# Fewer and longer dummy matmuls, an earlier first chunk, and a scale group moved into a K step, in the opening of a DiT block

## The chip, the cores and the metric

One core of one Trainium2 chip. The metric is the time of one execution in device microseconds. Timed runs come in rounds with the kernel before on the same chip.

## The reference

A DiT block with adaptive layer norm; only its first lines matter here.

```python
B, N, D = 2, 256, 1152
mod = (_silu(c) @ w_mod).reshape(B, 6, 1, D)
shift_a, scale_a, gate_a, shift_m, scale_m, gate_m = [mod[:, i] for i in range(6)]
h = _layernorm(x, axis=-1) * (1 + scale_a) + shift_a
qkv = (h @ wqkv).reshape(B, N, 3, H, Dh)
# [...] attention, wo, gated residual, second layer norm, MLP
```

## The kernel before

Tokens are four tiles of 128 (tiles 0 and 1 are batch 0, tiles 2 and 3 are batch 1). The opening normalizes them, transposes them on the tensor engine in chunks of 128 features ("chunk k"), multiplies each chunk by its scale (hT0), and accumulates six panels of K chunk by chunk ("K step k"). The scales come from small matmuls ("scale groups") on columns of w_mod that arrive by transfers in five pieces. Dummy matmuls on zeros keep the tensor engine busy until data is there.

```python
    zeros = const.tile([P, T], BF16, name="zeros")          # T = 512
    nc.vector.memset(zeros[:], 0.0)
    # [...]
    SGROUPS = [(0, 2), (2, 4), (4, 6), (6, 8), (8, 9)]
    for k0, k1 in SGROUPS:                # transfers, in this order on one queue
        nc.sync.dma_start(w_scale_a[:, :, k0 * P:k1 * P], ...)
        for a, z in [(0, 1), (1, 2)] if k0 == 0 else [(k0, k1)]:
            load_k(a, z, 0, KM1 * P)      # rows of w_k
    # [...]
    zeros32 = zeros[:].bitcast(FP32)      # 256 fp32 columns
    def warm(n, dst):
        for _ in range(n):
            nc.tensor.matmul(dst[:, 0:T // 2], zeros32[:, 0:P], zeros32, start=True, stop=True)
    warm(2, pwarm)
    nc.tensor.transpose(pc[:], c_sb[:], ident[0:B * KD, 0:B * KD])     # c, for the silu
    # [...]
    warm(8, pwarm)
    # [...] statistics: tiles 0 and 2 on ScalarE, 1 and 3 on VectorE
    pm0, pm1 = [scale_group(k, k + 1, acc_tile) for k in range(2)]
    act_var(2)                                                         # VectorE
    nc.vector.tensor_scalar_mul(hT0[:, 0, 0:N], pt_a[:, 0, :], pm0[:, 0, 0:1])
    scale_add(pm1, 1, 2, "a")
    modulate(pt_a, 1, 1, 0, 0, "d")
    ln_exp_rsqrt(rstd1[:, 2:3], mv1[:, 2, 1:2])                        # ScalarE
    nc.scalar.copy(scale_a[:, 0:1, :], pm0[:])
    norm1(2, 0, CUT)                                                   # VectorE
    # [...]
    k_step(0, 0, N)                        # K step 0, batch 0: six 128x256
    transpose_x([0, 1], [2], pt_c, 0)      # tile 2, chunks 0 and 1
    k_step(1, 0, N)
    modulate(pt_c, 0, 0, 1, 0, "d")        # chunk 0 of batch 1
    # [...]
    k_step(0, N, T)                        # K step 0, batch 1
    pm = scale_group(2, 4)
    # [...]
    for k in range(3, KD):
        if k in (3, 5, 7):
            k1 = min(k + 3, KD)
            scale_add(scale_group(k + 1, k1), k + 1, k1)
        if k < KD - 1:
            both(transpose_x([k + 1], range(NT)), k + 1)   # VectorE, then ScalarE
        k_step(k)                          # six 128x512
```

## Time and profile before

| | before |
|---|---|
| timed runs, median (lowest to highest) | 243.22 us (243.17 to 243.69), 3 runs |
| the profiled execution | 244.21 us, span 242.4 us |
| tensor engine busy | 98% of the span |
| its wait for w_scale_a columns 6-7 | 0.64 us |
| that transfer: issued, landed | 11.08 us, 19.77 us |

The page of the kernel before: its busy line, and the chain that ended last (shares of the span, by engine and by line).

```profile
span 242.4 us, 3999 instructions
...
PE 237.1 (98%) x1701; PEld 145.0 (60%) x1701; DVE 91.4 (38%) x193; ACT 59.6 (25%) x120; POOL 28.9 (12%) x48
...
PE 91%; SPq 4%; DMA 4%; issue 0%; DVE 0%; DVEq 0%
```

The chain is tensor work except for 8%: a transfer and the queue that issued it. The table of waits of the tensor engine in the first 30 us (waiting line, releaser: total us, times, longest; here its two longest) names the place.

```profile
PE pwarm L173 <- DVE eps_t L93: 1.2, 1, 1.2
PE pm L245 <- DMA w_scale_a<-in_w_mod_dram: 0.6, 1, 0.6
```

The timeline of the tensor engine of the kernel before (start, duration, line, operation, count, idle time before it). L173 are the dummies, L262 transposes, L278 K steps, L245 scale groups. It is put together from three stretches; the last, from 17.3 us, was asked up to 22.6 us, so its last line counts three of six matmuls.

```profile
1.18 2.07 PE L173 MATMUL pwarm<-zeros 128*128 128x256 f32 x4 [1.18 <-DVE eps_t L93]
3.18 0.19 PE L176 MATMUL pc<-ident,c_sb 18*128 18x18 bf16 x1
3.30 5.14 PE L173 MATMUL pwarm<-zeros 128*128 128x256 f32 x16
8.63 0.38 PE L262 MATMUL pt<-ident,xn 128*128 128x128 bf16 x4 [0.19 <-ACT xn L204]
...
10.42 0.82 PE L278 MATMUL pk<-big,w_k 128*128 128x256 bf16 x6
11.22 0.28 PE L262 MATMUL pt<-ident,xn 128*128 128x128 bf16 x2
11.34 1.49 PE L278 MATMUL pk<-big,w_k 128*128 128x256 bf16 x12
12.67 0.59 PE L245 MATMUL pm<-sT,w_scale_a 128*128 128x2 bf16 x18
...
17.73 1.46 PE L278 MATMUL pk<-big,w_k 128*128 128x512 bf16 x6
19.82 0.60 PE L245 MATMUL pm<-sT,w_scale_a 128*128 128x2 bf16 x18 [0.64 <-DMA w_scale_a<-in_w_mod_dram]
20.29 0.38 PE L262 MATMUL pt<-ident,xn 128*128 128x128 bf16 x4
20.50 1.46 PE L278 MATMUL pk<-big,w_k 128*128 128x512 bf16 x6
21.80 0.39 PE L262 MATMUL pt<-ident,xn 128*128 128x128 bf16 x4
22.02 0.81 PE L278 MATMUL pk<-big,w_k 128*128 128x512 bf16 x3
```

From 10.42 to 12.67 (the second scale group) nothing waits. The wait at 19.82 is the one that the change aims at. Last, the transfer of columns 6-7 in the view of transfers (size, us from issue to landing):

```profile
w_scale_a<-in_w_mod_dram SPq DMA_DIRECT2D x1, 576.0 KB, 8.7
```

### The profile page before, as it was taken

How to read it: one execution, taken by the hardware profiler on the slowest of the kernel's cores; microseconds unless marked ns; L12 is line 12 of the kernel's file. 1: busy time of each engine (PE TensorE's matmuls, PEld its weight loads, DVE VectorE, ACT ScalarE, POOL GpSimd, SP SyncE). 2: the span in 40 equal slices, each digit the busy share in tenths (PEclk: the TensorE clock that was granted, in tenths of full speed). 3: DMA queues.
4: the chain of work that ended last, by engine and by line, in shares of the span. 5: the costliest groups of instructions: out<-in, count | busy, mean ns of one | idle time of the engine just before them, and what ended most of it. 6: DMA issues, size and time to landing. Idle time of an engine off the chain costs nothing.

```text
span 242.4 us, 3999 instructions
## 1 busy us (share of the span) xinstructions
PE 237.1 (98%) x1701; PEld 145.0 (60%) x1701; DVE 91.4 (38%) x193; ACT 59.6 (25%) x120; POOL 28.9 (12%) x48
## 2 busy tenths in 40 slices
PE   8998999999999999999999999999999999999994
PEld 5675454465567665888854444444656656655674
DVE  4742442318416578831002999960010000000001
ACT  6622332307215032671422233322000000000000
POOL 2400000001400333200000000001121111111111
PEclk9999999999999999999999999999999999999999
DMA  6999999996499999239999999999300000000000
GB/s 184 325 317 318 376 366 391 390 392 236 107 314 398 388 374 145 40 62 351 390 391 392 342 327 290 271 326 286 97 16 16 20 16 16 20 16 17 29 22 16
DMA packets 48781, 53.29 MB, mean 220 GB/s; under 512 B 9587, under 2 KB 36475, under 8 KB 48763
## 3 DMA queue, kind: packets, MB, share of 16 engines
q1 hardware_dynamic: 41312, 50.14, 62.2%
q10 hardware_dynamic: 6939, 1.71, 5.1%
q0 software_dynamic: 512, 1.19, 1.8%
q8 instruction: 13, 0.21, 0.4%
q14 instruction: 5, 0.04, 0.1%
HBM read 50.14 MB, written 1.19 MB: 212 GB/s over the span
## 4 chain that ended last, share of the span: by engine, by line
PE 91%; SPq 4%; DMA 4%; issue 0%; DVE 0%; DVEq 0%
PE pacc L732 29%; PE pacc L788 29%; PE pacc L679 7%; PE pacc L588 7%; PE pq L510 7%; DMA w_scale_a<-in_w_mod_dram 4%; SPq L104 3%; PE pk L307 2%; PE pk L278 2%; PE pa L628 2%; PE ps_s L545 2%; PE pn L405 2%; SPq L86 1%; SPq L107 1%; PE pg L487 0%; PE pm L245 0%
## 5 line engine op out<-in xcount | busy, mean ns | idle before, releaser
L732 PE MATMUL pacc<-hT,w_f 128*128 128x256 bf16 (+1 forms) x432 | 70.5, 326 | 0.0
L788 PE MATMUL pacc<-w_f,gT 128*128 128x384 bf16 (+2 forms) x468 | 70.5, 314 | 0.0
L788 PEld LDWEIGHTS <-gT 128*128 128x128 bf16 x468 | 44.4, 98 | 26.3
L732 PEld LDWEIGHTS <-w_f 128*128 128x128 bf16 x432 | 42.2, 98 | 27.6
L794 DVE TENSOR_TENSOR tmp<-pacc,gate 128x384 f32<-128x384 f32 (+2 forms) x13 | 6.9, 527 | 65.6 <-PE pacc L788 57.2
L764 ACT ACTIVATE gT<-pacc 128x512 bf16<-128x512 f32 x24 | 14.3, 597 | 32.6 <-PE pacc L732 32.6
L458 DVE SCALAR_TENSOR_TENSOR part<-w_gate_m,s,part 128x1152 f32<-128x1152 bf16 x16 | 21.4, 1412 | 0.0
L796 POOL TENSOR_TENSOR o_sb<-tmp,x 128x384 bf16<-128x384 f32 (+1 forms) x12 | 11.7, 972 | 54.1 <-DVE tmp L794 54.1
L679 PE MATMUL pacc<-w_o,big 128*128 128x384 bf16 x108 | 17.9, 326 | 0.0
L510 PE MATMUL pq<-hT,w_q 128*128 128x512 bf16 x81 | 17.8, 379 | 0.0
L588 PE MATMUL pacc<-w_v,hT 128*128 128x384 bf16 x108 | 17.7, 326 | 0.0
L588 PEld LDWEIGHTS <-hT 128*128 128x128 bf16 x108 | 10.5, 98 | 7.1 <-issue 0.3
L679 PEld LDWEIGHTS <-big 128*128 128x128 bf16 x108 | 10.4, 98 | 7.2 <-issue 0.4
L510 PEld LDWEIGHTS <-w_q 128*128 128x128 bf16 x81 | 7.8, 97 | 9.5
L278 PE MATMUL pk<-big,w_k 128*128 128x256 bf16 (+1 forms) x72 | 13.2, 326 | 0.0
L685 POOL TENSOR_TENSOR x<-tmp,x_sb 128x384 f32<-128x384 f32 x8 | 7.3, 913 | 27.1 <-DMA w_scale_m<-in_w_mod_dram 15.2
L456 DVE TENSOR_SCALAR part<-w_gate_m,s 128x1152 f32<-128x1152 bf16 x2 | 1.6, 818 | 22.1 <-DMA w_gate_m<-in_w_mod_dram 22.1
L480 POOL DMA_DIRECT2D gates_dram<-nat_v x2 | 1.1, 536 | 67.7 <-DVE nat_v L478 67.7
L278 PEld LDWEIGHTS <-w_k 128*128 128x128 bf16 x72 | 6.7, 98 | 3.7 <-issue 0.3
L753 ACT ACTIVATE gT<-pacc 128x512 bf16<-128x512 f32 x12 | 6.5, 598 | 9.1 <-PE pacc L732 9.1
L173 PE MATMUL pwarm<-zeros 128*128 128x256 f32 x20 | 7.2, 527 | 1.2 <-DVE eps_t L93 1.2
L501 POOL DMA_DIRECT2D gates_dram<-nat x4 | 2.3, 586 | 50.6 <-DVE nat L498 49.9
(101 smaller groups left out, 165.9 us busy)
## 6 DMA issues: line engine op xcount, KB each, us to landing
w_f<-in_w_fc_dram SPq DMA_DIRECT2D x12, 864.0 KB, 14.6
w_f<-in_w_fc_dram SPq DMA_DIRECT2D x3, 1728.0 KB, 7.8
w_f<-in_w_fc_dram SPq DMA_DIRECT2D x2, 2592.0 KB, 17.2
w_gate_a<-in_w_mod_dram SPq DMA_DIRECT2D x3, 864.0 KB, 11.8
w_v<-in_wqkv_dram SPq DMA_DIRECT2D x3, 864.0 KB, 13.9
w_o<-in_wo_dram SPq DMA_DIRECT2D x3, 864.0 KB, 14.0
w_shift_m<-in_w_mod_dram SPq DMA_DIRECT2D x3, 864.0 KB, 8.6
w_scale_m<-in_w_mod_dram SPq DMA_DIRECT2D x3, 864.0 KB, 13.4
```

Of the source, the lines that this page charges most:

```text
L104: nc.sync.dma_start(w_k[:, k0:k1, c0:c1], wqkv_v[:, k0:k1, D + c0:D + c1])
L173: nc.tensor.matmul(dst[:, 0:T // 2], zeros32[:, 0:P], zeros32, start=True, stop=True)
L278: nc.tensor.matmul(pk[m][:, c0:c1], w_k[:, k, m * P:(m + 1) * P], hT0[:, k, c0:c1], start=(k == 0 and c0 == 0), stop=(k == KD - 1), skip_g ...
L458: nc.vector.scalar_tensor_tensor(part[:, b, :], wg[:, k, :], s32[:, k, b:b + 1], part[:, b, :], op0=ALU.mult, op1=ALU.add,)
L510: nc.tensor.matmul(pq[m][:], w_q[:, k, m * P:(m + 1) * P], hT[:, k, :], start=(k == 0), stop=(k == KD - 1), skip_group_check=True,)
L588: nc.tensor.matmul(pacc[:], hT[:, k, t * P:(t + 1) * P], w_v[:, k, pnl * PW:(pnl + 1) * PW], start=(k == 0), stop=(k == KD - 1),)
L679: nc.tensor.matmul(pacc[:], aT[:, k, t * P:(t + 1) * P], w_o[:, k, c0:c1], start=(k == 0), stop=(k == KD - 1),)
L685: (nc.gpsimd if pool_add else nc.vector).tensor_tensor(x1[:, t, c0:c1], tmp[:], x_sb[:, t, c0:c1], op=ALU.add)
L732: nc.tensor.matmul(dst, w_f1[m // KD][:, k, ml * P:(ml + 1) * P], hT[:, k, c0:c1], start=start, stop=(k == KD - 1), **kw,)
L764: nc.scalar.activation(gT[:, m, :], pacc[:], ACT.Gelu_apprx_tanh)
L788: nc.tensor.matmul(pacc[:], gT[:, kk, t * P:(t + 1) * P], w_f2[j][:, r, c0 - n * PW:c0 - n * PW + cw], start=(kk == 0), stop=(kk == KF - 1),)
L796: (nc.vector if last else nc.gpsimd).tensor_tensor(o_sb[:], tmp[:], x1[:, t, c0:c0 + cw], op=ALU.add)
```

## The change

Three parts, all in the opening. Five fp32 dummies of 512 columns in place of ten of 256. Chunk 0 of batch 0 multiplied ahead of tile 2's variance on VectorE, which idled there; with it, tile 2's transposes go behind K step 1. Two matmuls of K step 5 ahead of scale group 6-7, to fill the wait for its transfer.

```diff
-    zeros = const.tile([P, T], BF16, name="zeros")
-    nc.vector.memset(zeros[:], 0.0)
+    zeros32 = const.tile([P, T], FP32, name="zeros32")
+    nc.vector.memset(zeros32[:], 0.0)
+    zeros = zeros32[:, 0:T // 2].bitcast(BF16)
 [...]
-            nc.tensor.matmul(dst[:, 0:T // 2], zeros32[:, 0:P], zeros32, start=True, stop=True)
-    warm(2, pwarm)
+            nc.tensor.matmul(dst[:], zeros32[:, 0:P], zeros32[:], start=True, stop=True)
+    warm(1, pwarm)
 [...]
-    warm(8, pwarm)
+    warm(4, pwarm)
 [...]
+    nc.vector.tensor_scalar_mul(hT0[:, 0, 0:N], pt_a[:, 0, :], pm0[:, 0, 0:1])
     act_var(2)
-    nc.vector.tensor_scalar_mul(hT0[:, 0, 0:N], pt_a[:, 0, :], pm0[:, 0, 0:1])
 [...]
     k_step(0, 0, N)
+    k_step(1, 0, N)
     transpose_x([0, 1], [2], pt_c, 0)
-    k_step(1, 0, N)
 [...]
     for k in range(3, KD):
+        split = 2 if k == 5 else 0
+        k_step(k, 0, T, 0, split)
         if k in (3, 5, 7):
 [...]
-        k_step(k)
+        k_step(k, 0, T, split, KM1)
```

More of the change, by code (lines that the diff above doesn't have):

```diff
@@ L166 @@
     pwarm = acc_tile([P, T], "pwarm")
-    zeros32 = zeros[:].bitcast(FP32)
     def warm(n, dst):
         for _ in range(n):
-            nc.tensor.matmul(dst[:, 0:T // 2], zeros32[:, 0:P], zeros32, start=True, stop=True)
-    warm(2, pwarm)
+            nc.tensor.matmul(dst[:], zeros32[:, 0:P], zeros32[:], start=True, stop=True)
+    warm(1, pwarm)
     nc.tensor.transpose(pc[:], c_sb[:], ident[0:B * KD, 0:B * KD])
@@ L320, in fill @@
         for _ in range(n):
-            nc.tensor.matmul(pwarm[:], zeros[:, 0:P], zeros[:], start=True, stop=True)
+            nc.tensor.matmul(pwarm[:], zeros[:, 0:P], zeros, start=True, stop=True)
     def pool_eps(t):
```

## The prediction

> **What bounds the kernel.** The tensor engine: PE is 98% busy on the page, and the chain of waits, followed back, is unbroken tensor work from 19.82 us to 239.3. Before that it leaves the engine: 8.69 us for the transfer of w_scale_a columns 6-7 (issued 11.08, landed 19.77), and the transfer queue's issues before it. The table of waits gives the tensor engine 0.64 us idle there (timeline: K step 4 ends near 19.18, scale group 6-7 starts 19.82). So time saved before 19.2 us only lengthens this wait; only what moves work into it is gained.
>
> **What the change does.**
>
> 1. Dummies. Ten fp32 128x256 become five 128x512: the same columns. In the trace each is two records, 0.427 us apart at first and 0.216 us from about 6.5 us on. This agrees with the Trainium skill, "TensorE: Matmul & The Clock Gate", Part 1: half-rate clock until a free-running window of about 3.4 us was busy. The zero tile now has 512 fp32 words, not 256. Its memset took 0.27 us; I estimate 0.54, so the first dummy starts near 1.45, not 1.18, and the transpose of c, behind one long dummy, 0.1-0.15 us later; batch 0's statistics slip as much. Worth nothing by itself.
>
> 2. Chunk 0 ahead of tile 2's variance. VectorE idled 0.58 us before that variance (9.94; it waits for ScalarE until 9.91); chunk 0's multiply started at 10.02. It can start near 9.65, so K step 0 of batch 0 starts near 10.05, not 10.42. The variance comes up to 0.1 us later. Tile 2's transposes now stand after batch 0's step 1, but batch 1's first chunk still waits for variance, Ln, Exp, normalization, transposes, multiply: step 0 of batch 1 near 12.1, not 12.03. So the tensor engine gets a new gap of about 0.5 us just before 12 us, where this gain ends. Ahead of the transfer wait: worth about 0.
>
> 3. Scale group 6-7 inside step 5. Two of step 5's six 128x512 matmuls go ahead of the group. Their operands are there (chunk 5 multiplied by 18.79; w_k rows landed). The chain shows six in 1.29 us, 0.216 each: 0.43 us of the wait is filled, and step 5's rest behind the landing is that much shorter. Part is given back: step 5's tail and the next transposes now end near 21.6, while chunk 6 (VectorE, then ScalarE; ready 21.58 before, tied to the landing) comes near 21.65. I expect a new wait of 0.05-0.1 us before step 6.
>
> **Later transfers.** All needs come 0.4 us earlier. Tightest: the last 864 KB of w_k, landed 25.4, needed near 26.1 (then 25.7); scale columns 8, landed 22.2, needed 22.7. They hold, narrowly.
>
> **Sum.** 0.43 - 0.07 = about 0.35 us: 243.22 to **242.85 us**. Range 242.35 to 243.35 (8 in 10); the three runs before already differ by 0.5 us. Faster by over 2%: 0.01; within 2%: 0.98; slower: 0.01.
>
> **What would show it.** Right: group 6-7 still starts near 19.8, with two matmuls of step 5 before it and 0.1-0.2 us idle; step 6 starts near 21.65, not 22.02; everything behind is shifted evenly; a new gap just before 12 us. Wrong: group 6-7 starts later than the landing, because the head slipped by more than 0.2 us.
>
> **What would make it wrong.** The landing of w_scale_a moving by tenths between runs, which is as large as the effect; the clock coming up a window later because the dummies start later; the w_k tail landing after its new need; a larger wait before step 6, as VectorE and ScalarE multiply the halves one after the other.

## The result, and the profile after

| | before | after |
|---|---|---|
| timed runs, median (lowest to highest) | 243.28 us (243.15 to 243.69), 6 runs | 243.98 us (243.81 to 244.15), 6 runs |
| ratio after/before, 95% interval | | 1.0027 (1.0014 to 1.0040) |
| span of the profiled execution | 242.4 us (a run of 244.21) | 242.3 us (a run of 244.09) |

A ratio is the mean time of one kernel's runs over that of the other's of the same rounds, so it is not quite the ratio of the medians quoted. The class is "same" at 2%, but the time lies above the range that I gave: slower by 0.7 us where 0.35 us faster was predicted. The two profiled spans, which are what I had argued from, agree to 0.1 us.

The page of the kernel after, the same lines:

```profile
span 242.3 us, 3969 instructions
...
PE 236.6 (98%) x1681; PEld 143.0 (59%) x1691; DVE 91.6 (38%) x193; ACT 59.3 (24%) x120; POOL 28.9 (12%) x48
...
PE 98%; DVE 1%; issue 0%; DVEq 0%
```

The transfer is gone from the chain; it is tensor work back to the dummies, but for 0.36 us in which VectorE multiplies chunk 0 of batch 1. The tensor engine's waits:

```profile
PE pwarm L172 <- DVE eps_t L94: 1.4, 1, 1.4
PE pk L277 <- DVE big L267: 0.5, 1, 0.5
```

The tensor engine's timeline of the kernel after, asked for the same stretches (L172 dummies, L261 transposes, L277 K steps, L244 scale groups):

```profile
1.44 2.08 PE L172 MATMUL pwarm<-zeros 128*128 128x512 f32 x2 [1.44 <-DVE eps_t L94]
3.45 0.19 PE L175 MATMUL pc<-ident,c_sb 18*128 18x18 bf16 x1
3.57 5.69 PE L172 MATMUL pwarm<-zeros 128*128 128x512 f32 x8
9.10 0.39 PE L261 MATMUL pt<-ident,xn 128*128 128x128 bf16 x4
...
10.53 1.47 PE L277 MATMUL pk<-big,w_k 128*128 128x256 bf16 x12
11.84 0.28 PE L261 MATMUL pt<-ident,xn 128*128 128x128 bf16 x2
12.63 0.81 PE L277 MATMUL pk<-big,w_k 128*128 128x256 bf16 x6 [0.52 <-DVE big L267]
13.28 0.59 PE L244 MATMUL pm<-sT,w_scale_a 128*128 128x2 bf16 x18
...
18.33 1.89 PE L277 MATMUL pk<-big,w_k 128*128 128x512 bf16 x8
20.06 0.59 PE L244 MATMUL pm<-sT,w_scale_a 128*128 128x2 bf16 x18
20.51 0.38 PE L261 MATMUL pt<-ident,xn 128*128 128x128 bf16 x4
20.73 1.03 PE L277 MATMUL pk<-big,w_k 128*128 128x512 bf16 x4
21.59 0.39 PE L261 MATMUL pt<-ident,xn 128*128 128x128 bf16 x4
21.87 1.02 PE L277 MATMUL pk<-big,w_k 128*128 128x512 bf16 x3
```

Three readings. The gap before K step 0 of batch 1 is there (0.52 us at 12.63), and from 10.53 to the second scale group it is now 2.75 us, not 2.25. The eight matmuls at 18.33 are step 4 and the two from step 5, and scale group 6-7 starts at 20.06 without any wait. From that group to K step 6 it is 1.81 us, not 2.20: the split shortens what follows by 0.39 us, but the group itself starts 0.24 us later than in the trace before, not at the same time. Its transfer had landed long before:

```profile
w_scale_a<-in_w_mod_dram SPq DMA_DIRECT2D x1, 576.0 KB, 7.2
```

Issued at 11.37, it landed at 18.59, against 19.77 in the trace before. Nothing in the change touches this transfer. So the premise of the prediction, that this wait is there to be filled, was in doubt; and the dummies ended at 9.26 instead of 8.44, because they had started 0.26 us later and the full clock came at 7.61 us instead of 6.21. (A trace also records when the tensor engine's clock rises to full speed. In before, the dummies' records stand 0.427 us apart until then and 0.216 us apart soon after.)

### The profile page after: what moved, and what is told of

It is laid out like the page before. It is cut to its first block, busy times and chain, and to the rows that moved or that the text cites. A ratio compares the mean times of both kernels' runs of the same rounds, so it can differ in the third digit from the quotient of the medians.

```text
span 242.3 us, 3969 instructions
## 1 busy us (share of the span) xinstructions
PE 236.6 (98%) x1681; PEld 143.0 (59%) x1691; DVE 91.6 (38%) x193; ACT 59.3 (24%) x120; POOL 28.9 (12%) x48
## 4 chain that ended last, share of the span: by engine, by line
PE 98%; DVE 1%; issue 0%; DVEq 0%
PE pacc L789 29%; PE pacc L733 29%; PE pacc L680 7%; PE pacc L589 7%; PE pq L511 7%; PE pk L277 5%; PE pwarm L172 3%; PE pk L306 2%; PE pa L629 2%; PE ps_s L546 2%; PE pn L406 2%; PE pt L261 1%; PE pm L244 1%; PE pg L488 0%; DVE zeros L89 0%
## 5 line engine op out<-in xcount | busy, mean ns | idle before, releaser
L277 PE MATMUL pk<-big,w_k 128*128 128x256 bf16 (+1 forms) x70 | 12.9, 324 | 0.6 <-DVE big L267 0.5
L277 PEld LDWEIGHTS <-w_k 128*128 128x128 bf16 x72 | 6.8, 98 | 4.1 <-issue 0.6
L172 PE MATMUL pwarm<-zeros 128*128 128x512 f32 x10 | 7.8, 929 | 1.4 <-DVE eps_t L94 1.4
```

Of the source, the lines that this page charges most:

```text
L172: nc.tensor.matmul(dst[:], zeros32[:, 0:P], zeros32[:], start=True, stop=True)
L277: nc.tensor.matmul(pk[m][:, c0:c1], w_k[:, k, m * P:(m + 1) * P], hT0[:, k, c0:c1], start=(k == 0 and c0 == 0), stop=(k == KD - 1), skip_g ...
```

## The experiments

Twelve runs were made in three sessions, four kernels at a time on one chip (chip 12, then twice chip 2), each with five rounds beside the kernel before (6 timed runs of each, 11 of before; all correct; for transposes_back five runs). The three sessions' medians of before were 243.62, 243.82 and 243.64 us.

| run | parts | median us (lowest to highest) | ratio to before (95%) |
|---|---|---|---|
| dummies_only | long dummies | 243.72 (243.37 to 244.25) | 0.9996 (0.9978 to 1.0013) |
| chunk0_only | early chunk 0 and late transposes | 243.98 (243.58 to 244.39) | 1.0004 (0.9987 to 1.0021) |
| split_only | split of step 5 | 243.74 (243.17 to 244.15) | 0.9994 (0.9976 to 1.0011) |
| no_dummies | all but the long dummies | 244.07 (243.64 to 244.26) | 1.0004 (0.9986 to 1.0022) |
| after_again | the change | 243.75 (243.74 to 244.42) | 1.0007 (0.9995 to 1.0019) |
| transposes_back | the change, old transposes' place | 243.57 (243.40 to 243.87) | 0.9994 (0.9982 to 1.0006) |
| early_and_split | early chunk 0 and split | 243.67 (243.34 to 244.21) | 1.0001 (0.9987 to 1.0015) |
| transposes_only | late transposes | 244.32 (243.66 to 244.62) | 1.0021 (1.0008 to 1.0034) |
| late_scale | later transfer | 244.41 (244.30 to 244.86) | 1.0025 (1.0006 to 1.0044) |
| late_scale_split | later transfer and split | 244.27 (244.03 to 244.63) | 1.0016 (0.9997 to 1.0035) |
| after_third | the change | 243.95 (243.80 to 244.28) | 1.0005 (0.9986 to 1.0023) |
| transposes_back_2 | as transposes_back | 243.78 (243.54 to 244.00) | 0.9995 (0.9975 to 1.0015) |

Most intervals hold 1. Runs of before alone spread from 243.15 to 244.60 over the sessions, so times alone settle little. What settles more is that the traces, 14 with the two first, repeat to hundredths where no transfer is waited for. I read four marks in each from the tensor engine's timeline: the start of scale group 0-1 (G0), of scale group 2-3 (G1), of scale group 6-7 (G3), and of the last matmul of all (END).

| trace | G0 | G0 to G1 | G1 to G3 | columns 6-7 landed | G3 | G3 to END |
|---|---|---|---|---|---|---|
| before | 9.20 | 3.47 | 7.15 | 19.77 | 19.82 | 219.23 |
| dummies_only | 9.67 | 3.50 | 6.35 | 18.82 | 19.52 | 219.22 |
| split_only | 9.49 | 3.40 | 7.26 | 20.10 | 20.15 | 218.85 |
| chunk0_only | 9.75 | 3.83 | 6.35 | 18.94 | 19.94 | 219.31 |
| no_dummies | 9.49 | 3.85 | 6.78 | 18.62 | 20.12 | 218.84 |
| after | 9.52 | 3.76 | 6.78 | 18.59 | 20.06 | 218.84 |
| after_again | 9.22 | 3.76 | 6.78 | 17.87 | 19.75 | 218.84 |
| after_third | 9.69 | 3.77 | 6.78 | 18.83 | 20.24 | 218.84 |
| transposes_only | 9.40 | 4.01 | 6.35 | 18.55 | 19.76 | 219.22 |
| transposes_back | 9.30 | 3.50 | 6.78 | 18.50 | 19.59 | 218.84 |
| transposes_back_2 | 9.35 | 3.46 | 6.78 | 18.45 | 19.59 | 218.84 |
| early_and_split | 9.44 | 3.41 | 6.78 | 18.43 | 19.64 | 218.84 |
| late_scale | 9.44 | 3.54 | 7.03 | 19.97 | 20.01 | 219.23 |
| late_scale_split | 9.49 | 3.40 | 7.48 | 20.32 | 20.37 | 218.85 |

Where columns 6-7 landed early, G1 to G3 is 6.35 us without the split and 6.78 with it. In all 14 traces the measured time of the traced execution is END (G3 plus the last column) plus 5.14 to 5.20 us, so these marks account for the differences in time, not only for those in the opening.

### dummies_only

```diff
-    zeros = const.tile([P, T], BF16, name="zeros")   # and warm(2), warm(8) of 256 columns
+    zeros32 = const.tile([P, T], FP32, name="zeros32")   # and warm(1), warm(4) of 512 columns
```

> Before with only the five 128x512 dummies. Theory A (clock): the long dummies, or their later start, bring the full clock at about 7.85 us instead of 6.45, so the dummies end near 9.2 instead of 8.44 and the tensor engine, which in most runs of before waits for no transfer, is late by it: slower by 0.5 to 0.8 us, nearly the whole loss. Theory B (order): the loss comes from tile 2's transposes standing behind K step 1: within 0.15 us of before, clock up at about 6.5 us. Theory C (luck of the free-running window): the clock's rise differs from run to run whatever the dummies are: same as before on average, with a larger spread.

Measured: 0.9996, no loss that the times show. The full clock came at 4.78 us, not at 7.6, and the dummies ended at 7.86. Theory A falls: long dummies need not bring a late clock. The clock's rise came anywhere from 4.78 to 7.80 us over the 13 traces that recorded it (ten-dummy kernels 5.20 to 7.80, five-dummy ones 4.78 to 7.61), and the spread is the only part of theory C that holds.

### chunk0_only

```diff
+    nc.vector.tensor_scalar_mul(hT0[:, 0, 0:N], pt_a[:, 0, :], pm0[:, 0, 0:1])
     act_var(2)
-    nc.vector.tensor_scalar_mul(hT0[:, 0, 0:N], pt_a[:, 0, :], pm0[:, 0, 0:1])
...
     k_step(0, 0, N)
+    k_step(1, 0, N)
     transpose_x([0, 1], [2], pt_c, 0)
-    k_step(1, 0, N)
```

> Before with only the order of VectorE and of tile 2's transposes changed. Theory A: within 0.15 us of before, clock up at about 6.5 us. Theory B: slower by 0.4 to 0.6 us, with a wait of about 0.5 us before K step 0 of batch 1. Theory C: no difference, or luck.

Measured: 1.0004, inconclusive as a time. The trace shows the gap that theory B named, 0.52 us, and G0 to G1 at 3.83 us against 3.40 to 3.54 in every trace with the old order: 0.3 to 0.45 us lost.

### split_only

```diff
     for k in range(3, KD):
+        split = 2 if k == 5 else 0
+        k_step(k, 0, T, 0, split)
...
-        k_step(k)
+        k_step(k, 0, T, split, KM1)
```

> Before with only two matmuls of K step 5 ahead of scale group 6-7. My prediction's sum: faster by 0.35 us, if the 0.64 us wait for the transfer that the profile of before shows is in its timed runs too. If the profiled run of before was an odd one (244.2 us against 243.3 of the timed runs) and the transfer usually lands before it is needed, as it did in the profile of after: within 0.1 us.

Measured: 0.9994, 0.10 us faster by the means. That is nearer to the second outcome, but the interval reaches 0.35 us faster and so excludes neither; the trace says more. This trace was one of the two, of the twelve with the transfers in the old order, in which columns 6-7 landed late (20.10), and there the group waited in spite of the two matmuls ahead of it. The tensor engine's timeline of split_only:

```profile
17.94 1.89 PE L278 MATMUL pk<-big,w_k 128*128 128x512 bf16 x8
20.15 0.60 PE L245 MATMUL pm<-sT,w_scale_a 128*128 128x2 bf16 x18 [0.32 <-DMA w_scale_a<-in_w_mod_dram]
```

What follows the group took 218.85 us, against 219.22. In the other ten such traces the landing came at 17.87 to 18.94, before the group was reached.

### no_dummies

The changed kernel with the ten short dummies put back (the reverse of the diff of dummies_only).

> The changed kernel with the ten 128x256 dummies put back. Theory A: at before's time or up to 0.3 us faster; the loss is gone. Theory B: still slower by 0.4 us or more. Theory C: between, with a spread.

Measured: 1.0004, inconclusive as a time (the mean is 0.17 us above before's, near chunk0_only's 0.14); the interval holds theory A's outcome and theory B's. The trace has the gap before batch 1 still (0.52 us, G0 to G1 3.85 us).

### after_again

No edit to the changed kernel.

> The changed kernel unchanged, beside before once more. Theory D (the parts cancel): the order of chunk 0 and the transposes costs 0.2 us, the split gains 0.4 us only in runs where scale group 6-7 would have waited for its transfer, the dummies cost 0 to 0.15 us with the phase of the clock: within 0.3 us of before; the first verdict (slower by 0.65 us) was in good part the session. Rival (a real loss that no single part shows, as when late dummies and late transposes add up): again slower by 0.5 us or more.

Measured: 1.0007 (means 243.91 and 243.74 us): slower by 0.17 us, and the interval leaves out the 1.0027 of the first measurement, though the two intervals overlap. Theory D's guess, within 0.3 us, held.

### transposes_only

```diff
     k_step(0, 0, N)
+    k_step(1, 0, N)
     transpose_x([0, 1], [2], pt_c, 0)
-    k_step(1, 0, N)
```

> Before with only tile 2's transposes moved behind K step 1. Theory D: they wait for step 1 though their data is there: a gap of 0.5 to 0.8 us before K step 0 of batch 1, K step 4's end 12.3 to 12.7 us after x tile 2's landing, slower than before by 0.3 to 0.6 us. Rival (the early chunk's delay of the variance makes the gap, not the transposes): no gap, same time.

Measured: 1.0021 with an interval clear of 1: 0.5 us slower, the strongest single effect of the change's parts. The tensor engine's timeline of transposes_only:

```profile
10.66 1.47 PE L278 MATMUL pk<-big,w_k 128*128 128x256 bf16 x12
11.97 0.28 PE L262 MATMUL pt<-ident,xn 128*128 128x128 bf16 x2
12.76 0.71 PE L278 MATMUL pk<-big,w_k 128*128 128x256 bf16 x5 [0.51 <-DVE big L268]
```

Tile 2 was normalized by 11.42, but the engine, in order, ran K step 1 until 11.97; then transposes, multiply, and only then batch 1. G0 to G1 is 4.01 us. The rival falls: with the variance in its old place the gap is the same.

### transposes_back and transposes_back_2

The changed kernel with that one diff taken back; run in two sessions.

> The changed kernel with tile 2's transposes put back between K steps 0 and 1. Theory D: the 0.52 us gap before K step 0 of batch 1 falls to below 0.15 us; counted from the landing of x tile 2 the tensor engine finishes K step 4 after 11.9 to 12.05 us (before-like kernels 11.87 to 12.05 in four traces' three, reordered ones 12.16 to 12.23); faster than the changed kernel by 0.1 to 0.3 us. Rival: the gap stays, because the chain of variance, Ln, Exp and normalization is the limit and not the transposes' place: no difference.

> The changed kernel with tile 2's transposes in their old place, once more: faster than the changed kernel by 0.2 to 0.5 us, same as before to 0.3 us faster.

Measured: 0.9994 and 0.9995. Against the changed kernel in the same rounds the means are 243.59 to 243.91 and 243.76 to 244.02: faster by 0.32 and 0.26 us. The timeline of transposes_back:

```profile
10.31 0.85 PE L277 MATMUL pk<-big,w_k 128*128 128x256 bf16 x6
11.35 0.28 PE L261 MATMUL pt<-ident,xn 128*128 128x128 bf16 x2 [0.19 <-DVE xn L230]
11.47 1.49 PE L277 MATMUL pk<-big,w_k 128*128 128x256 bf16 x12
```

The gap is now 0.19 us (below 0.15 was expected), ahead of the transposes, and the twelve matmuls run through. G0 to G1 is 3.50 and 3.46 us, the value of the old order. One mark of my expectation did not work: the time from the landing of x tile 2 to the end of K step 4 (11.87 and 11.88 us here, as expected) was 12.73 in after_again and 12.52 in early_and_split, where x landed early, at 6.59 and 6.68. That landing is not always what the opening waits for, so I use G0 to G1 instead.

### early_and_split

Before with the early chunk 0 and the split, ten short dummies, the transposes in their old place.

> Before with chunk 0 ahead of the variance and the split of step 5, ten short dummies and the transposes in their old place: the version that the traces point to. Theory D: faster than before by 0.1 to 0.4 us, K step 4's end 11.9 to 12.05 us after x tile 2's landing. Rival: same as before, for the early chunk delays the variance.

Measured: 1.0001. It is no better than before; the rival's outcome, though G0 to G1 (3.41 us) shows no loss either. K step 0 starts 1.01 us after G0 instead of 1.22, but tile 2's chain, which starts elsewhere, decides when the next scale group is reached.

### late_scale and late_scale_split

To have the wait in every run, the transfer of columns 6-7 was issued after the rows 6-7 of w_k instead of ahead of them; the second kernel adds the split.

```diff
     for k0, k1 in SGROUPS:
+        if k0 == 6:
+            load_k(k0, k1, 0, KM1 * P)
         nc.sync.dma_start(w_scale_a[...])
+        if k0 == 6:
+            continue
```

> Before with the transfer of scale columns 6-7 issued after w_k rows 6-7 instead of ahead of them, so that it lands about 1.2 us later (near 19.7, in eight of ten traces it was 18.9 or earlier). Theory D (in most runs of before the group does not wait, for K step 4 ends at 19.0 to 19.5): now it waits nearly always: slower than before by 0.3 to 0.8 us. Rival (my prediction: before already waits 0.6 us in its usual run): slower by 1.0 us or more.

> The same late transfer with two matmuls of K step 5 ahead of the group. Theory D: the split's mechanism is right where there is a wait: faster than the late version without it by 0.35 to 0.43 us, group start to end 218.84 us as in every trace with the split against 219.22 without. Rival (the split is worthless even then, as something behind it waits): no difference between the two.

Measured: 1.0025 and 1.0016, means 244.52 and 244.29. The late transfer cost 0.65 us, inside theory D's 0.3 to 0.8 and below the rival's 1.0: this speaks against a usual wait of 0.6 us in before, though the interval, up to 1.07 us, does not quite exclude it. The split took back 0.23 us of it (0.35 to 0.43 expected); with six runs each, spread by about 0.2 us, that difference is not clear of noise. The timelines, late_scale first:

```profile
18.04 1.46 PE L282 MATMUL pk<-big,w_k 128*128 128x512 bf16 x6
20.01 0.60 PE L249 MATMUL pm<-sT,w_scale_a 128*128 128x2 bf16 x18 [0.52 <-DMA w_scale_a<-in_w_mod_dram]
```

and late_scale_split:

```profile
17.95 1.89 PE L282 MATMUL pk<-big,w_k 128*128 128x512 bf16 x8
20.37 0.60 PE L249 MATMUL pm<-sT,w_scale_a 128*128 128x2 bf16 x18 [0.54 <-DMA w_scale_a<-in_w_mod_dram]
```

In the second trace the transfer landed 0.35 us later than in the first and ate the gain of 0.38 us behind the group (218.85 against 219.23): the two ended together, at 239.2. The landing jitters by as much as the trick is worth.

### after_third

No edit, once more.

> The changed kernel once more, for the size of the loss. Theory D: slower than before by 0.1 to 0.3 us. Rival: by 0.5 us or more, as in the first measurement.

Measured: 1.0005 (means 244.02 and 243.87): slower by 0.15 us, as theory D had it.

## Why the prediction was wrong

**The step that failed** is the baseline: "So time saved before 19.2 us only lengthens this wait; only what moves work into it is gained." It took the 0.64 us wait of one profiled execution for the kernel's usual state. In ten of the twelve traces with the transfers in the old order, columns 6-7 landed at 17.87 to 18.94 us, before the tensor engine was there. From issue to landing the transfer took 7.2 to 7.3 us in these ten, and 8.7 us in the other two (before and split_only), with nothing between in the twelve: the wait came with a second, slower kind of landing, whose cause no run here shows. The profiled execution of before stood at 244.21 us, 1.0 us over the timed median, and I had both numbers when I predicted; I used the first for the mechanism and the second as the starting time, which took the wait's 0.6 us out of runs that mostly did not have it: of before's other 39 timed runs, only ten took more than 244.0 us.

**Part 3, the split.** "0.43 us of the wait is filled": the mechanism was right, the condition was not met. Where there is no wait, the two matmuls put the group 0.43 us later (G1 to G3, 6.35 to 6.78) and shorten what follows by 0.38 (219.22 to 218.84). The net is a loss of 0.05 us, the "new wait of 0.05-0.1 us before step 6" of the prediction, now with nothing to pay for it. Where the transfer is late the split is worth up to 0.38 us; the traces show that, the timed means (0.10 us faster alone, 0.23 us with a late transfer) only point that way.

**Part 2, the order.** "Ahead of the transfer wait: worth about 0." The predicted gap "of about 0.5 us just before 12 us" came out at 0.52 us. Without the transfer wait behind it, it is not absorbed. I had also missed its main cause: my numbers put the readiness of tile 2 (11.16 us before, up to 0.1 later) and the end of step 1 (10.05 and twice 0.65, about 11.35) close together, while in the trace after tile 2 is ready at 11.43 and the transposes start at 11.84. The early chunk alone is worth nothing (G0 to G1 3.41 to 3.50); the transposes' place alone costs 0.5 us (transposes_only); both together 0.2 to 0.45 us by the same marks.

**Part 1, the dummies.** "Worth nothing by itself" held as far as the times of dummies_only can show (0.9996). The first dummy came at 1.44 (predicted 1.45) and the transpose of c 0.27 us later (predicted 0.1 to 0.15), as the dummies ahead of it, the same columns in all, started 0.27 us later. Batch 0's first transposes start at 8.79 or 8.80 with an early clock, against 8.61 to 8.78 with the short dummies, and near 9.0 to 9.1 with a late clock under either. This reaches G0 only when the first scale columns have landed by then: it costs 0 to 0.2 us, depending on the run. The prediction's fear of "the clock coming up a window later because the dummies start later" was not borne out.

**The sum.** For a run that waits for no transfer the marks give 0.2 to 0.45 us for the order, 0.05 for the split and 0 to 0.2 for the dummies: slower by about 0.25 to 0.7 us. Measured by means: 0.66 (243.98 against 243.32), 0.17 and 0.15 us in three measurements. The sign is the same each time, though the intervals of the last two hold 1. The first measurement's before was faster than that of any later session (mean 243.32 against 243.74 to 243.87), and no run here shows why.

The fastest runs say more than the means. As an estimate from the marks, a run that waits for no transfer takes the first transpose plus 0.42 us (G0 in every trace where the columns were there), then G0 to G1, G1 to G3, G3 to END and 5.16 us. With the best values in the traces (first transposes at 8.61 and 8.80 us) this gives for before 9.03 + 3.40 + 6.35 + 219.22 + 5.16 = 243.16 us, and for the changed kernel 9.22 + 3.76 + 6.78 + 218.84 + 5.16 = 243.76. The fastest measured are 243.15 (of 39 runs) and 243.74 (of 18), and for the other seven kernels with the transfers in the old order the same sum comes within 0.12 us of the fastest run. So the change costs about 0.6 us where nothing waits: 0.36 for the order, 0.19 for the dummies, 0.05 for the split. In runs that do wait the difference should be smaller, as the split can help only runs that were already slow.

**A better version.** transposes_back beat the changed kernel in both sessions by about 0.3 us. Against before it is 0.06% and 0.05% faster, with intervals that hold 1: no gain over before is shown.

## What to carry to other kernels

Before you explain a wait in a profile, compare the profiled execution's time with the timed runs: if it is off by as much as the effect you are counting, the wait may belong to that execution alone, so look at it in several traces. Work put ahead of a wait is free only while the wait is there; otherwise it delays what stood behind it. On an engine that keeps the program's order, place a short instruction that heads a long chain (here two transposes, then a multiply) where its input becomes ready, not behind independent work that could have filled the chain's latency.

## What the Trainium skill lacked or had wrong

- "TensorE: Matmul & The Clock Gate", Part 1, says that the activity window is free-running and its phase changes from run to run. The traces agree: full clock at 4.78 to 7.80 us in near-identical openings. The page puts the transition near 4 us of matmuls, 0.5 us to either side; counted from the first dummy it was here 3.3 us (dummies_only) to 6.6 us (late_scale_split).
- The same page, Back-to-back issue gap, gives a sustained 131 ns per matmul of 512 columns in a real stream of weight loads and matmuls. Here such a stream keeps 216 ns (six in 1.29 us in the chain of waits of before), which is what the page gives for the isolated gap.
- No page says that a profile shows an fp32 matmul as two records. In these traces each fp32 dummy is two; at the full clock a record of 256 columns took 0.216 us and one of 512 took 0.43 us, so 512 fp32 columns cost 0.86 us, four times the 0.216 us of a bf16 matmul of 512 columns.
- No page says how far the landing of one transfer moves between executions: 576 KB of w_scale_a, in the same place of the same queue, landed 17.87 to 20.10 us into the span, 7.2 to 7.3 us after its issue in ten traces and 8.7 in two.
